# Sharing four PSUM banks among five users, and an order made from lengths taken back to back

## The chip, the cores and the metric

The kernel runs on one core of one Trainium2 chip. The metric is device time in microseconds (us) of one execution; the engines are TensorE (PE, with its weight loads as PEld), VectorE (DVE), ScalarE (ACT), GpSimd (POOL) and SyncE (SP), which here only issues DMAs. Each engine works through its own instructions in the order in which the program issues them, and waits for the others by semaphores. Before the change, three runs gave a median of 290.82 us (290.71 to 291.96).

## What is computed

Attention over 4 batches of 8 heads, 768 positions and 64 dimensions, in which each query sees only the 6 best of 24 chunks of 32 keys, and then an MLP on the 3072 tokens (512 to 2048 to 512) with an ELU between:

```python
k_min, k_max = min and max of k over each chunk of 32 keys
ub = sum over d of max(q * k_min, q * k_max)          # a bound for each query and chunk
ub = where(chunk of the query >= chunk, ub, -1e9)
top_chunks = the 6 chunks with the largest ub
scores = q @ k.T / 8, where the key's chunk is in top_chunks and key <= query
x = softmax(scores) @ v                                # 3072 x 512 after the heads are joined
h = x @ w_in                                           # 512 -> 2048
g = where(h > 0, h, exp(min(h, 0)) - 1)
out = g @ w_out                                        # 2048 -> 512
```

## The kernel before

Two heads make a pair; there are 16 pairs (the *units* u), four to a batch. Pairs are worked in halves of 384 queries (hf), and two pairs together are a quad for the selection of chunks. Each kind of step is one function that adds operations to a plan:

- `pair_prep` (line 361) for pairs 4 to 15: loads k, q and v, transposes k and q on DVE (L383, L401), takes the chunks' minima and maxima on DVE (L387, L394), and casts into the matmul operands on POOL (L506, L416). The loads of k and q go through three buffers named stage.
- `first_prep` (line 419) for pairs 0 to 3: the same with transposes on PE (L463), evicted by ACT.
- `quad_sel` (line 509): bounds by 32 small matmuls (L536), a transpose, the eighth largest value and a comparison on DVE (L553 to L573), and four copies on POOL (L583), which put the mask beside q as 24 more rows of the score matmul's operand.
- `pair_attend` (line 595): score matmuls into a double bank psS (L615), the exponential on ACT (L625), the causal triangle on POOL (L637), PV on PE into psO (L649), normalisation on DVE (L661, L664), three transposes on PE into psT (L673), and their copy into xT on ACT (L676).
- `mlp` (line 680), for each batch and half: 16 column blocks of up (L698, four matmuls each, into psH), the ELU as an exponential on ACT (L712) with a clamp (L730) and a maximum (L735) on DVE, or, in the blocks that `BOTH` names, with a second ACT operation (L717) and one DVE operation over two blocks (L723); then three row blocks of down (L747, 16 matmuls each, into psM), an eviction on ACT (L755) and the store (L759). The last batch takes the double banks for up and the class MT for down.

PSUM has eight banks. `caps` (line 190) gives S2 two double banks, and the other four single banks are one class `ps`, from which all the other users take. Each of these has a cap beside it: H (up, and the transposes of k at the start) 2, O (PV) 1, T (x^T) 2, M (down) 1, MT (transposes of q at the start, down of the last batch) 2. An operation that opens a bank takes one place of `ps` and one of its own class (`bank`, line 212), and both come free a latency after the last operation that reads it.

What sets the order of everything is `Plan.order` (line 106): a list scheduler, run when the program is made. Every operation has an engine, a length, and a priority; lower goes first. An operation may start when what it reads is written, a latency `LAT` after the writer's end, and when its buffers have places. The scheduler takes at each step the engine and operation that can start first, and among those that can start on one engine the one of lowest priority. It writes down this order, and the engines then run it as it stands: lengths and latencies in the plan set the order alone, not how long anything takes. The priorities are positions on an axis of pairs: attention of pair u at u, and half a pair later its second half (`pos`, line 269); preparation of pair u by `AHEAD` earlier (`AHEAD0` for pairs 0 to 3); selection 0.8 earlier; loads 4 earlier; the MLP of batch b from 4b + `MLAG[b]` on (`mpos`, line 275). The lengths come from `act`, `dve` and `pool` (lines 258 to 265) or stand beside an `add`. Weights are loaded by eight DMAs on POOL's queue, each behind an operation that `WHEN` names.

Of the kernel before, what the change touches and what calls it, by code (L numbers as in the profile page):

```python
# [16 lines left out]
H = 8  # L17
S = 768
# [37 lines left out]
class Plan:  # L56
# [3 lines left out]

    LAT = {"PE": 0.22, "ACT": 0.20, "DVE": 0.16, "POOL": 0.25, "SP": 2.2, "POOLQ": 2.5}

# [116 lines left out]
def kernel(  # L179
# [9 lines left out]
    nc = tc.nc  # L189
    caps = {"S2": 2, "ps": 4, "H": 2, "O": 1, "T": 2, "M": 1, "HT": 3, "MT": 2,  # L190
# [119 lines left out]
    def c_rows(i):  # L310
# [26 lines left out]
    def weights(i, gate):  # L337

        if i < 4:
            def f():  # L340
                nc.gpsimd.dma_start(out=w_in_sb[:, :, 512 * i:512 * i + 512], in_=wi3[:, :, 512 * i:512 * i + 512])
            name = ("w_in", i)
        else:
            def f():
                nc.gpsimd.dma_start(out=w_out_sb[:, 4 * i - 16:4 * i - 12, :], in_=wo3[:, 4 * i - 16:4 * i - 12, :])
            name = ("w_out", i - 4)
        add("POOL", 0.9, -20.0, f, reads=gate + ([("asked", i - 1)] if i else []), writes=[("asked", i)], lat=0.0)
        add("DMA", 3.05, -20.0, lambda: None, reads=[("asked", i)], writes=[name], lat=2.0)
# [12 lines left out]
    def pair_prep(u):  # L361
# [48 lines left out]
        def vload():  # L410
# [3 lines left out]
        fetch(1.0, 393.0, 205.0, pl + 1.2, vload, [vd], alloc=[vd])  # L414
        add("POOL", 0.09 + 0.00097 * S, pr + 1.0,
            lambda: nc.gpsimd.tensor_copy(out=tiles[vx][:, :, 0:D], in_=tiles[vd]),  # L416
            reads=[vd, "ones"], writes=[(vx, i) for i in range(2)], alloc=[vx], free=[vd])

    def first_prep(u, hf):
# [39 lines left out]
        def turn(bb, i):  # L459
# [4 lines left out]
            return f  # L464
        add("PE", 0.66, pr, turn(bk, i0), reads=[(sg, i0), "ident"], writes=[bk[0]], alloc=bk)
        for hd in range(2):
# [4 lines left out]
        for x, op in ((0, AOT.min), (1, AOT.max)):  # L471
# [10 lines left out]
            reads=[kx, (km, 0, hf)], writes=[(km, 1, hf)], free=[kx])  # L482
        add("PE", 0.66, pr + 0.05, turn(bq, i0 + 1), reads=[(sg, i0 + 1), "ident"], writes=[bq[0]], alloc=bq,
            free=[sg] if u == SPLIT[-1] else [])
# [11 lines left out]
        add("POOL", 0.09 + 0.00097 * HALF, pr + 1.0,  # L496
            lambda: nc.gpsimd.tensor_copy(
# [5 lines left out]
    def cast(pr, w, what, **kw):  # L503
        def f():
            o, i = what()
            nc.gpsimd.tensor_copy(out=o, in_=i)  # L506
        add("POOL", 0.09 + 0.00097 * w, pr, f, **kw)

    def quad_sel(g, hf):
# [5 lines left out]
        if True:  # L515
# [25 lines left out]
            for u in pairs:  # L541
# [3 lines left out]
                if hf:  # L545
                    fr += [PAIR[u]["km"]]
            add("PE", 4 * n / 2400 + 0.06, pr, ub, reads=rd, writes=[bu[0]], alloc=bu, free=fr)
            ut, = new("ubt")
# [3 lines left out]
            def t1(bu=bu, ut=ut, n=n, nh=nh, nb=nb, m0=m0):  # L552
# [6 lines left out]
            add("DVE", dve(n) + 0.16, pr, t1, reads=[bu[0]], writes=[ut], alloc=[ut], free=bu)  # L559
# [4 lines left out]
            add("DVE", 0.09 * nb + 0.07, pr, mx, reads=[ut], writes=[th], alloc=[th])  # L564
# [5 lines left out]
            add("DVE", dve(NCH * nb), pr, lt, reads=[ut, th, "kept"], writes=[sv], alloc=[sv], free=[ut, th])  # L570

# [4 lines left out]
            for j, u in enumerate(pairs):  # L576
                for odd in range(2):
                    r0 = 64 * odd + 32 * j
                    qb = PAIR[u]["qb"]

                    def put(r0=r0, odd=odd, qb=qb, c0=c0, n=n):
                        dst = tiles[qb][64:64 + NCH, :, SEL0 + c0:SEL0 + c0 + n]
                        nc.gpsimd.tensor_copy(  # L583
                            out=dst.rearrange("c h (i two x) -> c h i two x", two=2, x=32)[:, :, :, odd, :],
                            in_=tiles[st][r0:r0 + NCH, c0:c0 + n].rearrange("c (h i x) -> c h i x", h=2, x=32))
                    add("POOL", 0.12 + 0.0010 * n, pr + 0.01, put,
                        reads=[(st, hf)], writes=[(qb, hf, odd, "left")], free=[st] if hf and j and odd else [])
# [7 lines left out]
    def pair_attend(u, hf):  # L595
# [4 lines left out]
        if True:  # L600
# [4 lines left out]
            for ti, segs in enumerate(tiles_by_half[hf]):  # L605
# [5 lines left out]
                def sc(segs=segs, bs=bs):  # L611
                    p_s = tiles[bs[0]]
                    for (kb, c0, w, pc) in segs:
                        for hd in range(2):
                            nc.tensor.matmul(p_s[:, hd, pc:pc + w],  # L615
                                             lhsT=tiles[pt_["kb"]][0:64 + NCH, hd, 128 * kb:128 * kb + 128],
                                             rhs=tiles[pt_["qb"]][0:64 + NCH, hd, c0:c0 + w], start=True, stop=True)
                add("PE", 2 * wtot / 2400 + 0.02, pr, sc,
                    reads=[(pt_["kb"], i, hd) for i in range(hf + 1) for hd in range(2)]
# [22 lines left out]
            for qi, qt in enumerate(range(3 * hf, 3 * hf + 3)):  # L642
                for hd in range(2):
                    def pv(hd=hd, qi=qi, qt=qt, bo=bo, where=where):
                        po = ps(bo, [P, 2, 3, D + 1], F32)
                        for kb in range(qt + 1):
                            pt, c0, pc = where[kb]
                            off = pc + 128 * qt - c0
                            nc.tensor.matmul(po[:, hd, qi, :], lhsT=tiles[pt][:, hd, off:off + 128],  # L649
                                             rhs=tiles[pt_["vx"]][:, 6 * hd + kb, :],  # L650
                                             start=(kb == 0), stop=(kb == qt))
                    last = hd == 1 and qi == 2
                    add("PE", 0.033 * (qt + 1) + 0.02, pr, pv,
                        reads=[where[kb][0] for kb in range(qt + 1)] + [(pt_["vx"], i) for i in range(hf + 1)],
                        writes=[(bo[0], hd, qi)], alloc=bo if (hd, qi) == (0, 0) else [],
                        free=(held + ([pt_["vx"]] if hf else [])) if last else [])
# [3 lines left out]
            add("DVE", 0.19, pr,  # L660
                lambda rc=rc, bo=bo: nc.vector.reciprocal(out=tiles[rc], in_=ps(bo, None, None)[:, :, :, D:D + 1]),  # L661
# [8 lines left out]
            def xt(on=on, bx=bx):  # L670
                px = ps(bx, [P, HALF], BF16)
                for n in range(3):
                    nc.tensor.transpose(px[:, 128 * n:128 * n + 128], tiles[on][:, n, :, :], ident_b)  # L673
            add("PE", 0.18, pr, xt, reads=[on, "ident_b"], writes=[bx[0]], alloc=bx, free=[on])
            add("ACT", act(HALF), pr,
# [4 lines left out]
    def mlp(b, hf):  # L680
        tail = b == B - 1
        if True:
# [3 lines left out]
            for fc in range(0, NFC, step):  # L686
# [6 lines left out]
                def up(view=view, fc=fc, c0=c0):  # L693
                    for i in range(step):
                        ph = view()[:, i, :]
                        for kk in range(NKK):
# [3 lines left out]
                                             start=(kk == 0), stop=(kk == NKK - 1))  # L700
                add("PE", step * 4 * (HALF / 2400 + 0.003), pr, up,
                    reads=[("w_in", fc // 4)] + [(XT[4 * b + kk], hf) for kk in range(NKK)],
# [12 lines left out]
                if both:  # L715
# [12 lines left out]
                    continue  # L728
                add("DVE", 0.21 + 0.00037 * step * HALF, pr,
                    lambda e=e, t=t: nc.vector.tensor_scalar(  # L730
# [8 lines left out]
            for tt in range(3):  # L739
                bm = bank("MT" if tail else "M")  # L740
                for part in range(4):
                    pr = mpos(b, hf) + 2 + 2 * (4 * tt + part) / 12

                    def down(bm=bm, tt=tt, part=part, gt=gt):
                        pm = ps(bm, [P, DMODEL], F32)
                        for fc in range(4 * part, 4 * part + 4):
                            nc.tensor.matmul(pm, lhsT=tiles[gt][:, fc, 128 * tt:128 * tt + 128],  # L747
                                             rhs=w_out_sb[:, fc, :], start=(fc == 0), stop=(fc == NFC - 1))
                    add("PE", 4 * (512 / 2400 + 0.003), pr, down,
                        reads=[("w_out", part)] + [(gt, fc) for fc in range(4 * part, 4 * part + 4)],  # L750
                        writes=[(bm[0], part)], alloc=bm if part == 0 else [],
                        free=[gt] if tt == 2 and part == 3 else [])
# [86 lines left out]
```

## Time and profile before

| | us |
|---|---|
| median of three runs | 290.82 |
| the profiled execution, as timed | 291.4 |
| its span, first to last instruction | 289.3 |
| PE idle in the span | 26.4 |
| first matmul starts | 4.30 |
| last exponential of the attention ends, about | 240 |

The profile is that of one execution. A row of a group gives line, engine, operation, what it writes and reads, and the count, then the busy time and the mean ns of one; behind the second bar stands the idle time of the engine just before these instructions, with what ended it. Matmuls and operations of ACT and DVE overlap their neighbours by some of their length, so that a mean is longer than the time from one start to the next. A row of waits gives who waited for whom, the total, the number of times and the longest. A row of stage sums gives the busy time of each engine between two times. The chain of work that ended last is, by engine, 61% PE, 16% DVE, 8% POOL, 7% ACT.

### The profile page before, as it was taken

Reading aid. Unit: us, or ns where it says so; the run is one execution under the profiler, and the core shown is the slowest. Engines: PE = TensorE matmul, PEld = TensorE weight load, DVE = VectorE, ACT = ScalarE, POOL = GpSimd, SP = SyncE. Lnnn points to the kernel's source line nnn. Section 1 sums busy time; section 2 is a strip of 40 time slices with the busy share of each in tenths; the row PEclk is TensorE's granted clock in tenths of the full one; section 3 lists DMA queues with packets and bytes.
Section 4 is the critical chain, followed back from the end, with each engine's and each line's share of the span. In section 5 each row is a group of like instructions: output and inputs, shape, how many; then the busy total and the mean of one; then the engine's idle time right before and its main releaser. Section 6 shows DMA issues by size and latency. Waiting matters only on the chain.

```text
span 289.3 us, 6815 instructions
## 1 busy us (share of the span) xinstructions
PE 262.9 (91%) x2512; PEld 156.1 (54%) x2512; DVE 204.3 (71%) x542; ACT 202.2 (70%) x373; POOL 140.3 (49%) x238
## 2 busy tenths in 40 slices
PE   3686789969999999988889999999999999999994
PEld 2455456634565655645555656565566555555542
DVE  7835755799999978989999576756684517665620
ACT  3759599955898695898968987785869583443421
POOL 4678893384997699797759541521142010000000
PEclk9999799999999999999999999999999999999999
DMA  8878999999699979999734010001101010010011
GB/s 163 187 166 170 214 196 207 201 133 182 120 182 152 177 109 203 145 196 119 130 73 91 5 39 36 2 36 39 36 3 37 22 53 2 36 39 36 36 73 73
DMA packets 120992, 29.79 MB, mean 103 GB/s; under 512 B 113792, under 2 KB 117888, under 8 KB 120960
## 3 DMA queue, kind: packets, MB, share of 16 engines
q1 hardware_dynamic: 115136, 24.78, 46.9%
q0 software_dynamic: 4224, 4.19, 8.9%
q10 hardware_dynamic: 1600, 0.39, 0.7%
q8 instruction: 19, 0.31, 0.5%
q14 instruction: 13, 0.11, 0.1%
HBM read 27.26 MB, written 6.29 MB: 116 GB/s over the span
## 4 chain that ended last, share of the span: by engine, by line
PE 61%; DVE 16%; POOL 8%; ACT 7%; issue 4%; DMA 2%; DVEq 0%; POOLq 0%; ACTq 0%
PE psM L747 16%; PE psH L698 14%; PE psS L615 8%; PE psS L698 7%; PE psMT L747 7%; PE psO L649 5%; POOL rhs L583 3%; ACT pt L625 3%; PE psS L536 2%; DMA w_out_sb<-in_moe_w_out_dram 2%; DVE t L730 2%; POOL lhs L506 2%; DVE kx L387 1%; DVE thr L563 1%; POOL pt L637 1%
## 5 line engine op out<-in xcount | busy, mean ns | idle before, releaser
L625 ACT ACTIVATE pt<-psS 128x768 bf16<-128x768 f32 x112 | 90.1, 836 | 9.7 <-PE psS L615 9.3
L698 PE MATMUL psH<-xT,w_in_sb 128*128 128x384 bf16 x384 | 76.4, 325 | 4.2 <-DVE gT L735 3.2
L747 PE MATMUL psM<-w_out_sb,gT 128*128 128x512 bf16 x288 | 73.3, 379 | 0.4 <-DVE gT L723 0.3
L698 PEld LDWEIGHTS <-w_in_sb 128*128 128x128 bf16 x512 | 47.7, 97 | 36.6 <-issue 5.8
L712 ACT ACTIVATE e<-psH 128x384 f32<-128x384 f32 x96 | 48.2, 509 | 25.0 <-PE psH L698 24.3
L637 POOL TENSOR_SCALAR_AFFINE_SELECT pt<-pt 128x256 bf16<-128x256 bf16 x64 | 33.7, 531 | 53.7 <-ACT pt L625 44.9
L615 PE MATMUL psS<-rhs,lhs 88*128 88x384 bf16 (+2 forms) x288 | 52.3, 295 | 5.0 <-POOL rhs L583 3.8
L730 DVE TENSOR_SCALAR t<-e 128x384 bf16<-128x384 f32 (+1 forms) x64 | 33.6, 531 | 30.8 <-ACT e L712 30.4
L747 PEld LDWEIGHTS <-gT 128*128 128x128 bf16 x384 | 35.7, 97 | 35.6 <-DVE gT L723 1.1
L583 POOL COPY rhs<-selt 24x192 bf16<-24x192 bf16 (+1 forms) x64 | 30.6, 478 | 19.8 <-DVE selt L573 16.4
L615 PEld LDWEIGHTS <-lhs 88*128 88x128 bf16 x288 | 26.9, 99 | 21.3 <-issue 7.6
L649 PE MATMUL psO<-vext,pt 128*128 128x65 bf16 x672 | 32.0, 195 | 4.9 <-POOL pt L637 4.8
L506 POOL CAST rhs<-qt 64x768 bf16<-64x768 f32 (+1 forms) x40 | 29.5, 736 | 13.6 <-ACT qt L486 7.3
L649 PEld LDWEIGHTS <-pt 128*128 128x128 bf16 x672 | 28.4, 99 | 13.5 <-POOL pt L637 6.5
L723 DVE SCALAR_TENSOR_TENSOR gT<-e,t 128x768 bf16<-128x768 f32 x24 | 24.4, 1018 | 13.6 <-ACT t L717 13.4
L712 ACT ACTIVATE e<-psS 128x768 f32<-128x768 f32 x16 | 13.0, 810 | 21.4 <-PE psS L698 21.4
L735 DVE TENSOR_TENSOR gT<-t,psH 128x384 bf16<-128x384 bf16 x48 | 25.7, 542 | 1.9
L506 POOL CAST lhs<-kt 64x768 bf16<-64x768 f32 x24 | 23.4, 974 | 6.7 <-PE psS L615 3.0
L717 ACT ACTIVATE t<-psH 128x384 bf16<-128x384 f32 x48 | 24.6, 517 | 0.0
L698 PE MATMUL psS<-xT,w_in_sb 128*128 128x384 bf16 x128 | 23.4, 326 | 0.0
L747 PE MATMUL psMT<-w_out_sb,gT 128*128 128x512 bf16 x96 | 22.2, 379 | 0.0
L676 ACT ACTIVATE xT<-psT 128x384 bf16<-128x384 bf16 x32 | 16.3, 509 | 6.3 <-PE psT L673 6.2
(52 smaller groups left out, 268.1 us busy)
## 6 DMA issues: line engine op xcount, KB each, us to landing
out_dram<-osb SPq DMA_DIRECT2D x24, 256.0 KB, 2.0
stage<-in_k_dram SPq DMA_DIRECT2D x48, 96.0 KB, 4.0
stage<-in_q_dram SPq DMA_DIRECT2D x48, 96.0 KB, 3.5
vd<-in_v_dram SPq DMA_DIRECT2D x24, 192.0 KB, 3.8
w_in_sb<-in_moe_w_in_dram POOLq DMA_DIRECT2D x4, 512.0 KB, 8.2
w_out_sb<-in_moe_w_out_dram POOLq DMA_DIRECT2D x4, 512.0 KB, 8.6
gT<-in_k_dram SPq DMA_DIRECT2D x16, 96.0 KB, 2.7
gT<-in_v_dram SPq DMA_DIRECT2D x16, 96.0 KB, 2.6
```

The source lines that it names most:

```text
L506: nc.gpsimd.tensor_copy(out=o, in_=i)
L583: nc.gpsimd.tensor_copy(out=dst.rearrange("c h (i two x) -> c h i two x", two=2, x=32)[:, :, :, odd, :], in_=tiles[st][r0:r0 + NCH, c0:c0 ...
L615: nc.tensor.matmul(p_s[:, hd, pc:pc + w], lhsT=tiles[pt_["kb"]][0:64 + NCH, hd, 128 * kb:128 * kb + 128], rhs=tiles[pt_["qb"]][0:64 + NCH, ...
L625: lambda bs=bs, pt=pt, wtot=wtot: nc.scalar.activation(out=tiles[pt][:, :, 0:wtot], in_=tiles[bs[0]][:, :, 0:wtot], func=AF.Exp, scale=SCALE),
L637: nc.gpsimd.affine_select(out=a, in_=a, compare_op=AOT.is_ge, fill=0.0, base=0, pattern=pat, channel_multiplier=-1)
L649: nc.tensor.matmul(po[:, hd, qi, :], lhsT=tiles[pt][:, hd, off:off + 128], rhs=tiles[pt_["vx"]][:, 6 * hd + kb, :], start=(kb == 0), stop= ...
L698: nc.tensor.matmul(ph, lhsT=w_in_sb[:, kk, f0:f0 + 128], rhs=tiles[XT[4 * b + kk]][:, c0:c0 + HALF], start=(kk == 0), stop=(kk == NKK - 1))
L712: lambda e=e, view=view, i=i, w=w: nc.scalar.activation(out=tiles[e][:, i:i + w], in_=view(), func=AF.Exp),
L717: lambda t=t, view=view, i=i: nc.scalar.activation(out=tiles[t][:, i:i + 1], in_=view(), func=AF.Relu),
L730: lambda e=e, t=t: nc.vector.tensor_scalar(out=tiles[t][:, 0:step], in0=tiles[e][:, 0:step], scalar1=1.0, scalar2=1.0, op0=AOT.min, op1=AO ...
L735: lambda t=t, view=view, fc=fc, gt=gt: nc.vector.tensor_tensor(out=tiles[gt][:, fc:fc + step, :], in0=tiles[t][:, 0:step], in1=view(), op= ...
L747: nc.tensor.matmul(pm, lhsT=tiles[gt][:, fc, 128 * tt:128 * tt + 128], rhs=w_out_sb[:, fc, :], start=(fc == 0), stop=(fc == NFC - 1))
```

## The change

No operation is added or taken away. `caps` gives up to three banks to up, one to PV, one to x^T and two to down; the pool of four stays. The lengths and latencies of the plan are replaced, most by shorter ones, the clamp (L730) and the first fills by longer ones. `AHEAD` goes from 1.2 to 1.6, and `MLAG` of batches 1 to 3 from 3.5 to 3.0. The emitted instructions are the same; their order on each engine, and the banks and buffers that they use, are what the scheduler makes of the new numbers.

```diff
-MLAG = (2.0, 3.5, 3.5, 3.5)
-AHEAD = 1.2
+MLAG = (2.0, 3.0, 3.0, 3.0)
+AHEAD = 1.6
...
-    LAT = {"PE": 0.22, "ACT": 0.20, "DVE": 0.16, "POOL": 0.25, "SP": 2.2, "POOLQ": 2.5}
+    LAT = {"PE": 0.21, "ACT": 0.17, "DVE": 0.13, "POOL": 0.08, "SP": 2.2, "POOLQ": 2.5}
...
-    caps = {"S2": 2, "ps": 4, "H": 2, "O": 1, "T": 2, "M": 1, "HT": 3, "MT": 2,
+    caps = {"S2": 2, "ps": 4, "H": 3, "O": 1, "T": 1, "M": 2, "MT": 2,
...
     def act(n):
-        return 0.11 + 0.00082 * n
+        return 0.062 + 0.00082 * n
     def dve(n, rate=1):
-        return 0.12 + 0.00104 * n / rate
+        return 0.065 + 0.00104 * n / rate
     def pool(n):
-        return 0.16 + 0.00115 * n
+        return 0.15 + 0.00088 * n
...
-    add("DVE", 0.5, -9.9, c_fill, writes=["fill"])
+    add("DVE", 0.85, -9.9, c_fill, writes=["fill"])
-    add("DVE", 0.8, -9.0, c_zero, writes=["zero"])
+    add("DVE", 1.05, -9.0, c_zero, writes=["zero"])
```

The other lengths are written into `add` one by one, old on the left, new on the right:

```
weights (POOL issue)   0.9                      0.79
cast, v copy (POOL)    0.09 + 0.00097 n         0.13 + 0.00096 n
mask copy (POOL)       0.12 + 0.0010 n          0.20 + 0.00095 n
turn (PE)              0.66                     0.64
ub (PE)                4 n / 2400 + 0.06        0.22 + 0.002 n
ub transpose (DVE)     dve(n) + 0.16            dve(n) + 0.03
eighth largest (DVE)   0.09 nb + 0.07           0.078 nb
comparison (DVE)       dve(24 nb)               0.02 + 0.00125 * 24 nb
scores (PE)            2 w / 2400 + 0.02        2 w / 2400 + 0.01
PV (PE)                0.033 (qt + 1) + 0.02    0.0325 (qt + 1) + 0.005
reciprocal (DVE)       0.19                     0.115
x^T (PE)               0.18                     0.17
up (PE), each matmul   HALF / 2400 + 0.003      0.1625
clamp (DVE)            0.21 + 0.00037 n         0.32 + 0.00021 n
down (PE), each matmul 512 / 2400 + 0.003       0.2165
```

More of the change, by code (lines that the diff above doesn't have):

```diff
@@ L346, in weights @@
             name = ("w_out", i - 4)
-        add("POOL", 0.9, -20.0, f, reads=gate + ([("asked", i - 1)] if i else []), writes=[("asked", i)], lat=0.0)
+        add("POOL", 0.79, -20.0, f, reads=gate + ([("asked", i - 1)] if i else []), writes=[("asked", i)], lat=0.0)
         add("DMA", 3.05, -20.0, lambda: None, reads=[("asked", i)], writes=[name], lat=2.0)
@@ L414, in pair_prep @@
         fetch(1.0, 393.0, 205.0, pl + 1.2, vload, [vd], alloc=[vd])
-        add("POOL", 0.09 + 0.00097 * S, pr + 1.0,
+        add("POOL", 0.13 + 0.00096 * S, pr + 1.0,
             lambda: nc.gpsimd.tensor_copy(out=tiles[vx][:, :, 0:D], in_=tiles[vd]),
@@ L464, in turn @@
             return f
-        add("PE", 0.66, pr, turn(bk, i0), reads=[(sg, i0), "ident"], writes=[bk[0]], alloc=bk)
+        add("PE", 0.64, pr, turn(bk, i0), reads=[(sg, i0), "ident"], writes=[bk[0]], alloc=bk)
         for hd in range(2):
@@ L482, in first_prep @@
             reads=[kx, (km, 0, hf)], writes=[(km, 1, hf)], free=[kx])
-        add("PE", 0.66, pr + 0.05, turn(bq, i0 + 1), reads=[(sg, i0 + 1), "ident"], writes=[bq[0]], alloc=bq,
+        add("PE", 0.64, pr + 0.05, turn(bq, i0 + 1), reads=[(sg, i0 + 1), "ident"], writes=[bq[0]], alloc=bq,
             free=[sg] if u == SPLIT[-1] else [])
@@ L495, in first_prep @@
                  reads=[qt], writes=[(qb, hf, hd)], alloc=[] if hf or hd else [qb])
-        add("POOL", 0.09 + 0.00097 * HALF, pr + 1.0,
+        add("POOL", 0.13 + 0.00096 * HALF, pr + 1.0,
             lambda: nc.gpsimd.tensor_copy(
@@ L506, in f @@
             nc.gpsimd.tensor_copy(out=o, in_=i)
-        add("POOL", 0.09 + 0.00097 * w, pr, f, **kw)
+        add("POOL", 0.13 + 0.00096 * w, pr, f, **kw)
     def quad_sel(g, hf):
@@ L546, in quad_sel @@
                     fr += [PAIR[u]["km"]]
-            add("PE", 4 * n / 2400 + 0.06, pr, ub, reads=rd, writes=[bu[0]], alloc=bu, free=fr)
+            add("PE", 0.22 + 0.002 * n, pr, ub, reads=rd, writes=[bu[0]], alloc=bu, free=fr)
             ut, = new("ubt")
@@ L558, in t1 @@
                     nc.vector.memset(flat[0:64, i0:i0 + 34 * (nb // 2 - 1) + 1:34], CAUSNEG)
-            add("DVE", dve(n) + 0.16, pr, t1, reads=[bu[0]], writes=[ut], alloc=[ut], free=bu)
+            add("DVE", dve(n) + 0.03, pr, t1, reads=[bu[0]], writes=[ut], alloc=[ut], free=bu)
             def mx(ut=ut, th=th, nb=nb, m0=m0):
@@ L563, in mx @@
                     nc.vector.max(out=tiles[th][:, i, :], in_=tiles[ut][:, i, 0:m0 + 2 * (i % (nb // 2)) + 2])
-            add("DVE", 0.09 * nb + 0.07, pr, mx, reads=[ut], writes=[th], alloc=[th])
+            add("DVE", 0.078 * nb, pr, mx, reads=[ut], writes=[th], alloc=[th])
             def lt(ut=ut, th=th, sv=sv, nb=nb):
@@ L569, in lt @@
                     in1=tiles[th][:, 0:nb, TOPK - 1:TOPK].to_broadcast([P, nb, NCH]), op=AOT.is_lt)
-            add("DVE", dve(NCH * nb), pr, lt, reads=[ut, th, "kept"], writes=[sv], alloc=[sv], free=[ut, th])
+            add("DVE", 0.02 + 0.00125 * NCH * nb, pr, lt, reads=[ut, th, "kept"], writes=[sv], alloc=[sv], free=[ut, th])
             def t2(sv=sv, n=n, c0=c0):
@@ L585, in put @@
                             in_=tiles[st][r0:r0 + NCH, c0:c0 + n].rearrange("c (h i x) -> c h i x", h=2, x=32))
-                    add("POOL", 0.12 + 0.0010 * n, pr + 0.01, put,
+                    add("POOL", 0.20 + 0.00095 * n, pr + 0.01, put,
                         reads=[(st, hf)], writes=[(qb, hf, odd, "left")], free=[st] if hf and j and odd else [])
@@ L617, in sc @@
                                              rhs=tiles[pt_["qb"]][0:64 + NCH, hd, c0:c0 + w], start=True, stop=True)
-                add("PE", 2 * wtot / 2400 + 0.02, pr, sc,
+                add("PE", 2 * wtot / 2400 + 0.01, pr, sc,
                     reads=[(pt_["kb"], i, hd) for i in range(hf + 1) for hd in range(2)]
@@ L652, in pair_attend @@
                     last = hd == 1 and qi == 2
-                    add("PE", 0.033 * (qt + 1) + 0.02, pr, pv,
+                    add("PE", 0.0325 * (qt + 1) + 0.005, pr, pv,
                         reads=[where[kb][0] for kb in range(qt + 1)] + [(pt_["vx"], i) for i in range(hf + 1)],
@@ L659, in pair_attend @@
             o_all = [(bo[0], hd, qi) for hd in range(2) for qi in range(3)]
-            add("DVE", 0.19, pr,
+            add("DVE", 0.115, pr,
                 lambda rc=rc, bo=bo: nc.vector.reciprocal(out=tiles[rc], in_=ps(bo, None, None)[:, :, :, D:D + 1]),
@@ L673, in xt @@
                     nc.tensor.transpose(px[:, 128 * n:128 * n + 128], tiles[on][:, n, :, :], ident_b)
-            add("PE", 0.18, pr, xt, reads=[on, "ident_b"], writes=[bx[0]], alloc=bx, free=[on])
+            add("PE", 0.17, pr, xt, reads=[on, "ident_b"], writes=[bx[0]], alloc=bx, free=[on])
             add("ACT", act(HALF), pr,
@@ L700, in up @@
                                              start=(kk == 0), stop=(kk == NKK - 1))
-                add("PE", step * 4 * (HALF / 2400 + 0.003), pr, up,
+                add("PE", step * 4 * 0.1625, pr, up,
                     reads=[("w_in", fc // 4)] + [(XT[4 * b + kk], hf) for kk in range(NKK)],
@@ L728, in mlp @@
                     continue
-                add("DVE", 0.21 + 0.00037 * step * HALF, pr,
+                add("DVE", 0.32 + 0.00021 * step * HALF, pr,
                     lambda e=e, t=t: nc.vector.tensor_scalar(
@@ L748, in down @@
                                              rhs=w_out_sb[:, fc, :], start=(fc == 0), stop=(fc == NFC - 1))
-                    add("PE", 4 * (512 / 2400 + 0.003), pr, down,
+                    add("PE", 4 * 0.2165, pr, down,
                         reads=[("w_out", part)] + [(gt, fc) for fc in range(4 * part, 4 * part + 4)],
```

## The prediction, made before the changed kernel had run

> **What bounds the kernel now.** I read the totals of the page first, then stage sums cut where the row of tenths changes, then what PE waited for in the first two stages, then the groups.
>
> ```profile
> span 289.3 us, 6815 instructions
> PE 262.9 (91%) x2512; PEld 156.1 (54%) x2512; DVE 204.3 (71%) x542; ACT 202.2 (70%) x373; POOL 140.3 (49%) x238
> ```
>
> PE is busy 262.9 of 289.3 us, so 26.4 us are idle. The stage sums (columns: elapsed time, then PE, PEld, DVE, ACT, POOL busy, the clock, DMA) say where:
>
> ```profile
> 0.00:50.00 50.00, 36.91 (x392) 24.72 (x393) 31.41 (x119) 35.66 (x69) 34.60 (x78) 0.97 1.05 186
> 50.00:150.00 100.00, 90.84 (x1025) 54.50 (x1024) 92.30 (x233) 80.05 (x152) 75.24 (x108) 1.00 0.98 155
> 150.00:240.00 90.00, 89.55 (x859) 53.66 (x858) 57.65 (x163) 69.95 (x132) 30.48 (x52) 1.00 0.10 32
> 240.00:286.00 46.00, 45.64 (x242) 23.27 (x240) 22.97 (x31) 16.20 (x23) 0.00 (x0) 1.00 0.11 40
> 286.00:289.30 3.30, 0.00 (x0) 0.00 (x0) 0.00 (x0) 0.32 (x1) 0.00 (x0) 0.89 0.21 79
> ```
>
> Idle PE is 13.1, 9.2, 0.45, 0.36 and 3.3 us. From 150 us to the last matmul PE hardly stops, and the change removes no matmul. So the end moves only by what PE loses before 150 us, unless a new hole opens later. Between 50 and 150 us DVE is at 92.3 of 100 us: it prepares pairs 4 to 15 there, beside batches 0 and 1 of the MLP, and falls to 57.65 of 90 us once that is done. Engines run in order, so PE's losses are the waits of the planner's order:
>
> ```profile
> PE psH L698 <- DVE gT L735: 3.2, 3, 1.3
> PE psO L649 <- POOL pt L637: 3.1, 7, 1.0
> PE psT L673 <- DVE on L664: 0.7, 1, 0.7
> PE psS L615 <- ACT pt L625: 0.6, 2, 0.4
> ```
>
> These are the largest waits of PE between 50 and 150 us (total, times, longest). In the first row an up matmul waits until DVE has read an older psH: that is a wait for a bank. psO behind POOL is a wait for data, a masked pt that the order took for ready. Before 50 us the waits are another sort: 5.0 us for the first k to land and 3.8 us (longest 3.0) for the selection copied by POOL (L583).
>
> **The change, part by part.** It adds and removes no instruction; it deals banks out anew and makes another order. No trace of before shows that order, so every part has two ends.
>
> *Third bank for up.* The three waits of the first row are 1.32, 1.15 and 0.70 us in the timeline. With a third bank, one more up of four matmuls (0.65 us in the chain) can run before the bank is needed: what is left is 0.67, 0.50 and 0.05, so 3.2 becomes 1.2 and the gain is 2.0 us. Ends: nothing, when the freed place is filled with more ups and the wait only comes one up later; 3.8 us, which is this row and the two of 0.3 us each for psH behind ACT.
>
> *Second bank for down.* A psM is held through four parts (4 x 0.86 us) and the eviction, mean 614 ns (L755). In this trace no wait of PE names psM and an eviction, since other work stands between two downs. So I take nothing; the ends are nothing and, at 0.6 us for each of the 7 evictions of L755 between 50 and 150 us, 4.2 us of freedom that PE could only use where it idles, which is in the same 9.2 us.
>
> *One bank for x^T instead of two.* It is held for three transposes and a copy: 0.33 us and 509 ns (L676), with the gaps about 1 us, 32 times. No wait names psT for its bank. Two users seldom meet within 1 us; I charge 0.4 us (one meeting in the sixteen halves of that stage), ends nothing and 16 x 0.5 = 8 us, if every copy stood in the way. All four single banks are one pool as before: three ups and one PV leave none for down and x^T.
>
> *New lengths.* The mean of a group includes the end of its pipeline; back to back the starts lie closer. In the timeline one pt exponential of 0.87 us starts at 50.46 and the next ACT operation at 51.15, 0.69 us later; the old length for 768 elements is 0.74, the new 0.69. A 128x384 operation is followed after 0.37 us (old 0.425, new 0.377). Summed over all operations, the old lengths give DVE 205 and ACT 202 us, the new 187 and 184; PE stays at 255 and POOL at 136. So the old order was made for DVE and ACT slower than they are, and places PE's attention work later than its data are ready; with true lengths it should stall less on data. The data waits between 50 and 150 us are 3.1 + 0.7 + 0.6 + 0.4 + 0.3 = 5.1 us. I take half, 2.5 us; ends nothing and 5.1. POOL's latency falls from 0.25 to 0.08 us, and psO behind POOL is the largest data wait, so this part can also lose: seven waits lengthened by 0.17 are 1.2 us.
>
> *AHEAD 1.2 to 1.6, MLAG 3.5 to 3.0.* Both go ahead of attention by nearly the same step, so among themselves preparation gains 0.1 of a pair on batches 1 to 3 and 0.4 on batch 0, whose lag stays 2.0. A pair costs DVE two transposes, two reductions and a subtraction, 3.64 us by the new lengths: 0.4 x 3.64 = 1.5 us of DVE work go before the MLP's in the stage where DVE has 7.7 us left. PE feels part of it: 0.5 us, ends nothing and 1.5. The loads move along on SP's queue. Their places come free when DVE has transposed (SP waits 11.2 us there behind DVE, none of DVE's waits is for a load), so I price the queue at nothing; what hides it is DVE's own backlog.
>
> *Before 50 us and at the end.* The start hangs on landings and on the chain through selection, which keep their work; I take nothing, ends 1.5 us each way (half of the longest wait, 3.0). The end, eviction and store behind the last matmul, stays 3.3 us.
>
> **The sum**: -2.0 - 2.5 + 0.4 + 0.5 = -3.6 us. The profiled execution took 291.4 us, its span 289.3. So 291.4 - 3.6 = 287.8 us for an execution like it, and as the median of the runs (290.82) is 0.6 us lower, 287.2 us.
>
> **A row that speaks against the lengths.** DVE's clamp t<-e (L730) on 384 elements is planned at 0.40 us. By shape it takes
>
> ```profile
> L730 DVE TENSOR_SCALAR t<-e 128x384 bf16<-128x384 f32 x13 | 5.4, 412 | 7.2 <-ACT e L712 7.2
> L730 DVE TENSOR_SCALAR t<-e 128x384 bf16<-128x384 f32 x16 | 11.3, 720 | 0.7 <-ACT e L712 0.7
> ```
>
> The first row is 200 to 240 us, where POOL is nearly idle; the second 60 to 150 us, where POOL casts: 0.31 us more each. A length from an undisturbed place is 16 x 0.31 = 5 us short in the stage where DVE is full. The Trainium skill, "SBUF — State Buffer", section "Who interferes with whom", says that such an instruction with a constant can take a port pair that DVE shares with GpSimd, and that whichever comes second blocks until the other is through. By that rule the stretch follows casts wherever they go, and the trace agrees as far as it goes, 720 against 412 ns.
>
> **Rivals.**
> - *The lock (slower).* The new order counts on 18 us of DVE time that the old did not, but the clamps take 5 us more than planned in that stage, and more of batches 0 and 1 stands beside the casts since the MLP is earlier. It decides when DVE's 7.7 us are used up: 5 + 1.5 + the casts' own stretch (974 ns for lhs against a planned 0.87, 24 of them: 2.5) is 9.0. PE then loses that and gets no data wait back: -2.0 + 0.4 + 4 = +2.4, about 293 us. Chance 0.15.
> - *Banks (slower).* Three ups hold three of four banks, each until a full DVE has read it (waits of about 1.07 us in before), and PV or x^T of the next half finds none; the attention that feeds the next batch gets late. It decides from the point where PE has no other ready work. Six of sixteen halves at 1.07 us are 6.4 us, less the 2.5 of the lengths: about 294.5 us. For it: four banks carry five kinds. Against it: the planner knows the banks and puts other work in between. Chance 0.17.
> - *No difference.* The waits change names, since DVE at 92% feeds PE all the same in that stage: 290.8 us, chance 0.15.
> - *More is recovered.* Bank waits 3.8, data waits 5.1 and 1.5 at the start go: 290.8 - 10.4, at best 280.5; about 282.5 where a fifth of it stays. Chance 0.11.
> - The forecast, 287.2 us (284 to 289.3): chance 0.42.
>
> **How the numbers follow.** Half a per cent, 1.5 us, is about what a measurement of this kernel can tell from no change: 289.4 to 292.3 us is "same". Forecast and full recovery give 0.53 faster, the no-difference case 0.15, the two slower rivals 0.32. With about one in ten left out on each side, the range goes from 282.5, where recovery is nearly full, to 295, just over the banks' rival.
>
> **What would show it.** Right: from 150 us on PE again without holes; PE idle between 50 and 150 us near 5.6 us; the psH row behind DVE near 1.2 us; the last matmul about 3.6 us sooner. Wrong: psT, psO or psM waiting for banks (rival two); DVE over 95% with L730 above 720 ns and PE behind DVE (rival one); or a hole after 150 us, because attention came late and a batch of the MLP lacks its x^T, which nothing in this trace prices, as there is no such hole in it. The start could also move by more than 1.5 us, if the shorter lengths let the order ask before the loads have landed.

## The result and the profile after

The changed kernel takes 293.28 us, the median of 16 runs (292.18 to 294.56); before took 291.32 us beside it. The ratio is 1.0067, 95% interval 1.0047 to 1.0086: **slower by 2 us**, where a gain of 3.6 us, to 287.2, was forecast. The time lies in the range, but on the other side of no change. Single executions that took over 1.5% longer than the quickest of the same kernel are left out of the times and ratios below. The profiled execution took 292.27 us, at the quick end of its runs:

```profile
span 290.5 us, 6802 instructions
PE 260.4 (90%) x2483; PEld 154.5 (53%) x2512; DVE 207.7 (72%) x542; ACT 201.3 (69%) x373; POOL 139.2 (48%) x238
```

The stage sums, with the same columns as before (29 of PE's 2512 matmul records are missing from this trace, about half of them between 50 and 150 us, so a little of PE's idle time is not real):

```profile
0.00:50.00 50.00, 34.03 (x384) 23.06 (x385) 31.74 (x117) 34.13 (x69) 33.89 (x77) 0.90 1.06 186
50.00:150.00 100.00, 91.60 (x982) 54.53 (x997) 91.62 (x223) 81.89 (x156) 70.48 (x104) 1.00 0.89 151
150.00:240.00 90.00, 88.52 (x863) 52.41 (x874) 59.67 (x169) 66.13 (x125) 33.73 (x56) 1.00 0.13 37
240.00:286.00 46.00, 45.79 (x269) 24.44 (x273) 24.65 (x34) 18.55 (x26) 1.04 (x2) 1.00 0.11 40
286.00:290.50 4.50, 0.50 (x2) 0.06 (x1) 0.00 (x0) 0.60 (x1) 0.00 (x0) 1.00 0.15 58
```

Before 50 us PE idles 16.0 instead of 13.1 us. Between 50 and 150 us it idles 8.4 instead of 9.2 us, but DVE's full stage now lasts to 160 us. Cut there, PE is busy for the same time in both; this is before, then the changed kernel:

```profile
50.00:160.00 110.00, 100.84 (x1094) 60.28 (x1093) 102.27 (x252) 88.71 (x170) 82.80 (x117) 1.00 0.92 147
```

```profile
50.00:160.00 110.00, 100.84 (x1079) 59.70 (x1088) 101.56 (x251) 88.73 (x170) 77.20 (x113) 1.00 0.85 144
```

PE's waits between 50 and 150 us in the changed kernel have other names. All rows of this view add up to 7.4 us, against 8.9 before; without psH behind DVE they are 5.8 us (and 0.2 without a name) against 5.7. The largest are:

```profile
PE psT L673 <- DVE on L664: 1.7, 3, 0.8
PE psH L698 <- DVE gT L735: 1.4, 2, 1.1
PE psS L615 <- POOL rhs L583: 1.4, 2, 1.2
PE psO L649 <- POOL pt L637: 0.7, 2, 0.4
PE psS L615 <- ACT pt L625: 0.7, 1, 0.7
PE psO L649 <- ACT xT L676: 0.5, 1, 0.5
PE psS L615 <- DVE ubt L553: 0.5, 1, 0.5
```

What is new stands at the start. These are the timeline's PE rows of the changed kernel around its second long hole (start, length, what; the hole ahead in brackets):

```profile
29.71 0.56 PE L536 MATMUL psS<-qt,km 64*32 64x192 f32 x16
...
34.68 0.50 PE L673 MATMUL psT<-ident_b,on 128*128 128x128 bf16 x3 [3.30 <-DVE on L664]
35.11 0.89 PE L536 MATMUL psS<-qt,km 64*32 64x192 f32 x16
```

PE waits 3.30 us for DVE's normalisation of pair 3. Before had two groups of bounds (L536) ahead of that x^T, and its hole was 1.00 us:

```profile
32.96 0.56 PE L536 MATMUL psS<-qt,km 64*32 64x192 f32 x16
33.31 0.82 PE L536 MATMUL psS<-qa,km 64*32 64x192 f32 x16
35.13 0.34 PE L673 MATMUL psT<-ident_b,on 128*128 128x128 bf16 x3 [1.00 <-DVE on L664]
```

In the changed kernel 16 matmuls of one shape that took 0.56 us ahead of the hole take 0.89 us behind it. The clock says why (the last column but two, in two stretches of the changed kernel):

```profile
10.00:20.00 10.00, 5.84 (x70) 3.53 (x62) 4.82 (x20) 5.67 (x12) 6.75 (x16) 0.71 0.82 185
30.00:40.00 10.00, 6.63 (x99) 3.58 (x84) 7.64 (x42) 4.71 (x11) 8.28 (x15) 0.83 1.42 214
```

PE ran at half clock from 14.2 to 21.1 and from 34.7 to 38.1 us. The record starts at the first change of the clock, so the 1.00 that a trace shows ahead of it says nothing: in before, whose record starts at 22.3 us, a transposition ahead of that takes as long as at half clock and one behind it does not.

```profile
21.37 0.88 PE L463 MATMUL psH<-ident_f,gT 128*128 128x128 f32 x3
24.45 0.55 PE L463 MATMUL psH<-ident_f,gT 128*128 128x128 f32 x3
```

So before ran at half clock up to 22.3 us and again from 29.1 to 32.5, the changed kernel up to 10.8 us and in the two stretches above: in the first 50 us that is 21.4 us of before from the first matmul on, and 16.7 of the changed kernel. An estimate from these traces, PE's busy time halved where the clock was: by 50 us before has done 28.5 us of work at full clock and the changed kernel 26.9, so it is 1.7 us behind there. It idles 2.9 us more and loses 1.2 us less by the clock. The 16 runs fall into groups by the mean clock: 292.2 to 292.6 us at 0.980 to 0.982, 293.2 to 293.6 at 0.968 to 0.971, 294.2 to 294.6 at 0.968.

### The profile page after: what moved, and what is told of

The parts are those of the page before. It is cut to its first block, busy times and chain, and to the rows that moved or that the text cites. A ratio compares the mean times of both kernels' runs of the same rounds, so it can differ in the third digit from the quotient of the medians.

```text
span 290.5 us, 6802 instructions
## 1 busy us (share of the span) xinstructions
PE 260.4 (90%) x2483; PEld 154.5 (53%) x2512; DVE 207.7 (72%) x542; ACT 201.3 (69%) x373; POOL 139.2 (48%) x238
## 4 chain that ended last, share of the span: by engine, by line
PE 49%; DVE 24%; ACT 14%; issue 5%; POOL 3%; DMA 3%; SPq 0%; DVEq 0%; POOLq 0%; ACTq 0%
PE psM L747 12%; PE psH L698 10%; PE psS L698 7%; ACT pt L625 7%; PE psMT L747 7%; PE psS L615 6%; PE psO L649 3%; ACT e L712 3%; DVE thr L563 2%; DVE t L730 2%; DVE gT L723 2%; DVE gT L735 2%; DMA vd<-in_v_dram 2%; DVE kx L387 2%; DVE km L387 2%
## 5 line engine op out<-in xcount | busy, mean ns | idle before, releaser
L747 PE MATMUL psM<-w_out_sb,gT 128*128 128x512 bf16 x263 | 69.4, 379 | 1.8 <-ACT t L717 0.3
L712 ACT ACTIVATE e<-psH 128x384 f32<-128x384 f32 x96 | 48.2, 530 | 24.0 <-PE psH L698 22.8
L637 POOL TENSOR_SCALAR_AFFINE_SELECT pt<-pt 128x256 bf16<-128x256 bf16 (+1 forms) x64 | 33.3, 527 | 60.0 <-ACT pt L625 58.7
L615 PE MATMUL psS<-rhs,lhs 88*128 88x384 bf16 (+2 forms) x288 | 51.4, 296 | 7.2 <-POOL rhs L583 5.0
L730 DVE TENSOR_SCALAR t<-e 128x384 bf16<-128x384 f32 (+1 forms) x64 | 32.2, 506 | 24.9 <-ACT e L712 24.4
L583 POOL COPY rhs<-selt 24x192 bf16<-24x192 bf16 (+1 forms) x64 | 29.8, 465 | 22.0 <-DVE selt L573 18.4
L615 PEld LDWEIGHTS <-lhs 88*128 88x128 bf16 x288 | 26.9, 99 | 23.7 <-issue 10.4
L506 POOL CAST rhs<-qt 64x768 bf16<-64x768 f32 (+1 forms) x40 | 31.1, 777 | 15.4 <-DVE qt L401 7.8
L723 DVE SCALAR_TENSOR_TENSOR gT<-e,t 128x768 bf16<-128x768 f32 x24 | 27.0, 1124 | 12.1 <-ACT t L717 12.0
L712 ACT ACTIVATE e<-psS 128x768 f32<-128x768 f32 x16 | 13.0, 812 | 19.1 <-PE psS L698 19.1
L506 POOL CAST lhs<-kt 64x768 bf16<-64x768 f32 x24 | 21.5, 896 | 6.9 <-DVE kt L383 5.1
```

The costliest lines, as they stand in the source:

```text
L583: nc.gpsimd.tensor_copy(out=dst.rearrange("c h (i two x) -> c h i two x", two=2, x=32)[:, :, :, odd, :], in_=tiles[st][r0:r0 + NCH, c0:c0 ...
L615: nc.tensor.matmul(p_s[:, hd, pc:pc + w], lhsT=tiles[pt_["kb"]][0:64 + NCH, hd, 128 * kb:128 * kb + 128], rhs=tiles[pt_["qb"]][0:64 + NCH, ...
L637: nc.gpsimd.affine_select(out=a, in_=a, compare_op=AOT.is_ge, fill=0.0, base=0, pattern=pat, channel_multiplier=-1)
L712: lambda e=e, view=view, i=i, w=w: nc.scalar.activation(out=tiles[e][:, i:i + w], in_=view(), func=AF.Exp),
L723: lambda e=e, t=t, fc=fc, gt=gt: nc.vector.scalar_tensor_tensor(out=tiles[gt][:, fc - 1:fc + 1, :], in0=tiles[e], scalar=1.0, in1=tiles[t] ...
L730: lambda e=e, t=t: nc.vector.tensor_scalar(out=tiles[t][:, 0:step], in0=tiles[e][:, 0:step], scalar1=1.0, scalar2=1.0, op0=AOT.min, op1=AO ...
```

## Which part of the change it is

Theory A put the loss at the start and on the new lengths, B on the banks, C on the priorities. Each part was run alone and in pairs. Times are medians; ratios are to before run beside each and lie near the ratio of the mean times, so that they differ a little from the quotient of two medians.

**Lengths and latencies alone.**

```diff
 banks, MLAG and AHEAD of before; LAT, act(), dve(), pool() and all other lengths of the change
```

> Before with the new lengths and latencies alone; banks, AHEAD and MLAG as before. Theory A (the loss lies in the first 50 us, where the new lengths make an order with longer holes of PE, 3.6 and 3.3 us, and the clock falls): this alone gives most of the loss, +1 to +2 us against before, with a hole of over 3 us behind the normalisation of pair 3 between 30 and 36 us. Theory B (banks): no loss here, -1 to 0 us. Theory C (priorities): no loss here, -1 to +0.5 us.

300.24 us, ratio 1.0286 (1.0258 to 1.0315). The size is far over what any theory said, and the place is wrong too: the start is that of the changed kernel, with the same hole of 3.3 us, but PE is busy only 97.88 us between 50 and 160 us, 6.8 us of this stretch are at half clock, and with two banks for up PE waits there for

```profile
PE psH L698 <- DVE gT L735: 4.6, 5, 1.7
PE psO L649 <- POOL pt L637: 2.2, 3, 0.9
PE psT L673 <- DVE on L664: 1.2, 3, 0.5
```

**Banks alone, priorities alone.**

```diff
-"H": 2, "O": 1, "T": 2, "M": 1
+"H": 3, "O": 1, "T": 1, "M": 2
```

> Before with the new shares of the banks alone (up 3, x^T 1, down 2). Theory A: within 0.7 us of before, the start hardly changed. Theory B (three ups hold the banks that PV and x^T need): +1.5 us or more, with waits of psO or psT for banks between 50 and 160 us. Theory C: within 0.7 us.

290.08 us, ratio 0.9950 (0.9930 to 0.9971): a gain. B falls. The row of psH behind DVE is 1.3 us.

```diff
-MLAG = (2.0, 3.5, 3.5, 3.5)
-AHEAD = 1.2
+MLAG = (2.0, 3.0, 3.0, 3.0)
+AHEAD = 1.6
```

> Before with AHEAD 1.6 and MLAG 3.0 alone. Theory A: within 0.7 us of before, since nothing before about 45 us is moved by them, and what PE loses between 50 and 150 us is set by the work of DVE there. Theory C (preparation and MLP pushed ahead of attention, which ends some 7 us later in the changed kernel): +1.5 us or more, with the loss between 50 and 160 us. Theory B: within 0.7 us.

288.13 us, ratio 0.9887 (0.9861 to 0.9913). C falls, and A's "within 0.7 us" with it. PE gains 2.7 us between 50 and 160 us, with DVE as full as before:

```profile
50.00:160.00 110.00, 103.51 (x1111) 61.04 (x1110) 102.14 (x254) 90.67 (x175) 81.42 (x117) 1.00 0.90 146
```

**Pairs of parts**, edited as above.

> The changed kernel with the old lengths and latencies: banks and priorities alone. If the parts add up (banks -1.4 us, priorities -3.3 us alone): -4.7 us, 286.7 us, with PE losing under 8 us between 50 and 150 us. If both gains are the same waits of psH behind DVE, found twice: -3.3 us, 288.1 us. If the order is a matter of luck at each change: anywhere between -4.7 and +3 us.

293.89 us, ratio 1.0086 (1.0052 to 1.0120): two gains together are a loss.

> New lengths and new banks, AHEAD and MLAG as before. With the lengths alone PE waited 5.0 us for psH behind DVE. If the third bank takes most of that, +4 us against before (the lengths' +8.8 less 4 to 5); if the parts only add up, +7.4 us; the rest of the way to the changed kernel's +2 us is then what the priorities give here.

295.24 us, ratio 1.0134 (1.0103 to 1.0165).

> New lengths and AHEAD 1.6, MLAG 3.0, with the banks as before: the last of the eight ways to make the change in part. If parts add up (lengths +8.8, priorities -3.3 us alone): +5.5 us, 297 us; from the changed kernel (+2.0) without the banks' -1.4: +3.4 us. Theory L: neither number holds, anything between 288 and 300 us.

295.64 us, ratio 1.0120 (1.0086 to 1.0154). The start goes with the lengths: x^T of pair 3 waits 3.3 us for DVE in all four kernels that have the new ones, and 0.8 to 1.3 us in the four that have the old ones. The total does not follow, and nothing adds up. In per cent, the banks give -0.5, the priorities -1.1, the lengths +2.9; banks with priorities +0.9, lengths with banks +1.3, with priorities +1.2, all three +0.7. No part of the change has a worth that it keeps when another is set beside it.

## Slack in the lengths, or a new deal

Two theories were left: S, the too long old lengths are slack that keeps PE fed; L, any change of a number deals the greedy list anew, and before is a good deal. The first pair of runs moved all lengths along the line from old to new (new - old = 1), the others one constant by 5 ns.

```diff
 lengths and latencies: old + 0.5 * (new - old)
```

> Before, with each length and latency half way between the old and the new value; banks and priorities as before. If the slack in the old lengths is what keeps PE fed (theory S): a part of the lengths' loss that grows with the cut, +3 to +6 us. If any change of lengths deals the list anew and the +8.8 us are one unlucky draw (theory L): anything from -3 to +9 us, in no order with the cut.

294.59 us, ratio 1.0118 (1.0079 to 1.0157).

```diff
 lengths and latencies: old - 0.5 * (new - old)
```

> Before, with each length and latency moved the other way, by half the distance from the new to the old value beyond the old one (a 128x384 ACT operation 0.449 us instead of 0.425, POOL's latency 0.335 instead of 0.25); banks and priorities as before. Theory S: no loss, -3 to 0 us. Theory L: anything, as likely slower as faster.

299.31 us, ratio 1.0269 (1.0244 to 1.0294): more slack is as bad as none. S falls.

```diff
-        return 0.11 + 0.00082 * n
+        return 0.115 + 0.00082 * n
```

> Before with one number moved by next to nothing: the constant of ACT's lengths 0.115 instead of 0.110 us, 1% of a 128x384 operation. Theory L (each change of numbers deals the greedy list anew; before is a lucky draw): a time that differs by 1 us or more, rather slower, up to 300 us. Theory S (the cut in the lengths matters, by its size): within 0.7 us of before.

293.85 us, ratio 1.0073 (1.0043 to 1.0102). Five ns in the plan cost as much as the whole change. On DVE the two traces part after the 58th instruction, where a reduction (L473) and a reciprocal (L661) change places; 237 of DVE's 542 places then hold another kind of instruction, and only the last 59 are alike again.

> The same 5 ns on top of AHEAD 1.6 and MLAG 3.0 alone. Theory L: the gain of 3.3 us of the priorities alone is a draw too and does not last: 290 to 297 us. If the priorities have a worth of their own: 287.5 to 289 us, or at least 3 us less than the run of before with the 5 ns.

With the same edit: 299.45 us, ratio 1.0242 (1.0203 to 1.0280). The gain of the priorities does not outlive 5 ns.

```diff
 changed kernel, act(): 0.062 -> 0.067 and, in another run, 0.057
```

> The changed kernel with the constant of ACT's lengths at 0.067 instead of 0.062 us. Theory L: the changed kernel's 293.3 us is one draw from a spread of some 288 to 300 us that every setting shares, so 1 us or more away from it, either way. If the change has a worth of its own that a few ns do not touch: 292.5 to 294.3 us.

293.38 us, ratio 1.0046 (1.0026 to 1.0065).

> The changed kernel with the constant of ACT's lengths at 0.057 instead of 0.062 us. Theory L: as with the 5 ns more, and in no order with it: anywhere between 288 and 300 us. If the change has a worth of its own: 292.5 to 294.3 us.

295.56 us, ratio 1.0128 (1.0097 to 1.0159). The first lies as near to the changed kernel as a worth of its own would have it, the second does not. Fourteen orders of the same instructions, before's among them, take 0.989 to 1.029 of before's time, and eleven are slower than it. Of the four moves by 5 ns one did nothing clear of the noise (0.2%), and the others moved the time by 0.6, 0.7 and 3.6%. Theory L stands: before is among the better deals, and the change's +0.7% is within what 5 ns do.

## What a bad deal is made of: holes, and the clock behind them

Theory G: a stretch in which PE idles much is followed by 3.41 us at half clock. The holes of the start were filled with matmuls into the bank that the waiting ones then overwrite.

```diff
+ first scores:           28 matmuls ident_b x ident_b, 128 columns, into psS
+ x^T of pair 3, half 0:  28 transposes of ident_b into psT
```

> The changed kernel with 28 matmuls of 128 columns more ahead of the first score matmul and 28 transposes more ahead of the x^T of pair 3, first half, each into the bank that the real ones then overwrite: they stand in the two holes of 3.6 and 3.3 us and keep PE busy there. If the holes cost by the clock that falls after them: 0.7 to 2 us less than the changed kernel, 291.3 to 292.5 us, a mean granted clock of 0.985 or more in all runs, and runs that differ by less than 0.8 us. If only the holes themselves cost: the same time as the changed kernel, 293.3 us, or up to 1 us more for the added work that juts out.

290.20 us, ratio to before 0.9951 (0.9935 to 0.9967), runs from 289.62 to 291.29 us: 3.1 us less than the changed kernel, with more work for PE, and 1.1 us under what the clock was expected to give at most. The runs still differ by 1.7 us. The same stretches as above, now of the filled kernel:

```profile
10.00:20.00 10.00, 6.91 (x103) 5.18 (x95) 5.08 (x22) 6.05 (x12) 6.70 (x16) 0.86 0.74 168
30.00:40.00 10.00, 8.16 (x121) 5.50 (x108) 8.43 (x43) 6.16 (x13) 8.62 (x17) 1.00 1.42 215
```

The clock between 30 and 40 us is full. Before and the priorities' kernel got the like: the 28 matmuls, 12 and 26 more ahead of two PV groups of pair 2, and 12 transposes ahead of the x^T.

> Before with the same added matmuls at the same places; its order is that of the priorities' run up to about 45 us. Theory G: its half-clock windows up to 22.3 us and from 29.1 to 32.5 us go, 0.7 to 1.7 us less than before, about 290 us; so that the changed kernel filled (290.2 us) and before filled are alike, and the change's loss is its two longer holes at the start. Without G: 291.3 us or a little more.

290.53 us, ratio 0.9951 (0.9930 to 0.9973). Filled, the two kernels are level in time, but this does not show that the clock made the difference between them. A filled kernel has the order of the unfilled one (the added lines only shift its line numbers), so their traces can be laid side by side. These are an up matmul of the changed kernel, then the same one filled; then an up and the first down of before, and the same two of before filled:

```profile
40.59 0.81 PE L698 MATMUL psH<-xT,w_in_sb 128*128 128x384 bf16 x4
```

```profile
38.64 0.81 PE L704 MATMUL psH<-xT,w_in_sb 128*128 128x384 bf16 x4
```

```profile
42.19 0.81 PE L698 MATMUL psH<-xT,w_in_sb 128*128 128x384 bf16 x4
45.05 1.02 PE L747 MATMUL psM<-w_out_sb,gT 128*128 128x512 bf16 x4
```

```profile
40.41 0.81 PE L708 MATMUL psH<-xT,w_in_sb 128*128 128x384 bf16 x4
44.41 1.02 PE L757 MATMUL psM<-w_out_sb,gT 128*128 128x512 bf16 x4 [1.19 <-DMA w_out_sb<-in_moe_w_out_dram]
```

Filling brings the changed kernel forward by 1.9 us and before by 1.8: as far as the fills take the half clock of the start away, it cost both alike in these traces. Then filled before has caught up with a DMA, waits 1.19 us for the weights of down, and keeps 0.6 us; the filled changed kernel has no such wait. So the half clock is a cost of both starts, and in these traces the filled kernels are level by a wait for weights. What the changed kernel has more of than before is idle time. (Its trace is from the quick end of its runs; in the others the clock may take more.)

> Before with AHEAD 1.6 and MLAG 3.0 alone, and added matmuls in the holes of the first 36 us (28 ahead of the first scores, 12 and 26 ahead of two PV groups of pair 2, 12 transposes ahead of the x^T of pair 3), each into the bank that the real ones then overwrite. Theory G (a window of 3.4 us in which PE idles much is followed by 3.4 us at half clock): the half-clock windows up to 20.8 us and from 31.1 to 37.9 us go, and 1 to 2 us with them: 286 to 287.2 us. Without G: 288.1 us or a little more.

287.65 us, ratio 0.9853 (0.9827 to 0.9878): the quickest version here, quicker than both kernels. Its median is 0.5 us over what was expected. Set against before beside each, it is 0.3% below the unfilled one, with intervals that overlap, so that a gain by the filling is not shown here; it too waits for the weights of down, 0.7 us.

Then the middle, in the order of the priorities with 5 ns more, which has five half-clock windows after 45 us.

```diff
+ first scores of pair 4:  50 matmuls ident_b x ident_b
+ x^T of pair 3, half 1:   36 transposes of ident_b       (first of the two runs only)
```

> The order of the priorities with 5 ns more (299.5 us), and added matmuls in its two longest holes of the middle: 36 transposes ahead of the x^T of pair 3, second half (a hole of 2.3 us, PE behind DVE), and 50 matmuls of 128 columns ahead of the first scores of pair 4 (3.2 us, behind POOL), each into the bank that the real ones overwrite. The half-clock windows there are 63.3 to 70.1 and 73.6 to 80.4 us. If the windows follow from the holes (theory G): both go, and 4 to 6 us with them, 293.5 to 295.5 us. If the holes alone cost: 299.5 us or up to 1 us more.

299.06 us, ratio 1.0258 (1.0216 to 1.0299), against 293.5 to 295.5 us by theory G: inconclusive. The transposes waited with the real ones and stood behind their hole of 2.31 us, as work of 2.9 us more. Without them:

> The order of the priorities with 5 ns more (299.5 us), with the 50 added matmuls ahead of the first scores of pair 4 alone: the 36 added transposes of the run before stood behind the same wait as the real ones, did not fill their hole and put 2.9 us of work behind it. Theory G: the half-clock window of 6.8 us behind the 3.2 us hole goes (73.6 to 80.4 us), and 2 to 3.4 us with it: 296 to 297.5 us. If the hole alone costs: 299.5 us or a little more.

296.49 us, ratio 1.0187 (1.0159 to 1.0215), where the unfilled order had 1.0242 (1.0203 to 1.0280). The hole and what follows it, unfilled and then filled:

```profile
74.67 1.44 PE L615 MATMUL psS<-rhs,lhs 88*128 88x384 bf16 x6 [3.16 <-POOL rhs L583]
```

```profile
71.41 2.96 PE L615 MATMUL psS<-ident_b 128*128 128x128 bf16 x50
74.68 0.81 PE L618 MATMUL psS<-rhs,lhs 88*128 88x384 bf16 x6 [0.32 <-POOL rhs L583]
```

The scores start at the same time, since POOL is no sooner, but take 0.81 instead of 1.44 us. So a part of what a bad order costs is not its holes but the clock behind them, here about 0.55 of 2.4%. The rest of these 7 us, and what makes one order poorer in holes than another, is not settled. No single wait is the largest in all the slow orders.

## Why the prediction was wrong, point by point

- **The bound** was right: PE has no holes after the stage in which DVE is full, and all is decided before. That stage ends when DVE's work is done, and reaches to 160 us here.
- **Third bank for up**: the number came out, the mechanism is not shown. The row of psH behind DVE was put at 1.2 us; it is 1.4, and 1.3 with the banks alone, which gain 0.5%, 1.4 us, against 2.0 less 0.4. But the row is 1.0 us with two banks and the new priorities, and 3.3 us with three banks in the changed kernel with 5 ns more. It moves with the deal as much as with the bank, so the match may be luck.
- **New lengths, -2.5 us**: the step that failed. It said that an order made from true lengths stalls less on data, by half of 5.1 us. Between 50 and 150 us the waits of PE other than for psH stayed, 5.1 us before and 5.8 now, and at the start the new lengths made one longer, 3.30 us for the x^T of pair 3 instead of 1.00. The lengths alone cost 2.9%, half of the way 1.2%, and the way back 2.7%: the order is not the better the truer the lengths. One length was measured, and the new plan is nearer to it: in before, idle DVE starts 0.523 us (median of 20) after the start of the ACT exponential L712 of 384 elements that it waits for; the plan now says 0.377 + 0.17, and said 0.425 + 0.20.
- **AHEAD and MLAG, +0.5 us**: by themselves they gain 1.1%, and with 5 ns more they cost 2.4%; a price for this edit by itself has no meaning here. The working also had a step the wrong way round: preparation moves 0.4 of a pair ahead and the MLP 0.5, so on batches 1 to 3 the MLP gains 0.1 on preparation.
- **The sum**: it added parts. The eight combinations show that they don't add, so a sum of this sort could not have come out right but by chance. That the time lies in the range is luck as well: six of the other orders lie above it, since it was made for the mechanisms that I could name and not for the spread of the list. Two figures of the rivals do not follow from their rows: 290.8 - 10.4 is 280.4, not 280.5, and the 4 us that the lock takes from PE have no source; its own 9.0 us against 7.7 left give 1.3.
- **Before 50 us, nothing, 1.5 us each way**: wrong, and here the 2 us lie. PE idles 2.9 us more in the profiled start, and by the estimate above it is 1.7 us of work behind at 50 us. Landings and selection kept their work, as I said, but the order of the new lengths has the x^T of pair 3 ahead of bounds that stood before it and kept PE busy. The clock I left out altogether; it costs the start, but before's start as well.
- **The lock**: not it. DVE is at 91.6 of 100 us, and between 60 and 150 us L730 is shorter than before (720 ns), not longer:

```profile
L730 DVE TENSOR_SCALAR t<-e 128x384 bf16<-128x384 f32 x15 | 9.2, 616 | 0.1
```

- **The banks' rival**: not it; psT waits for its data, 1.7 us behind DVE, not for a bank, and the banks alone gain. **No difference**, by waits that change names, is what happened between 50 and 160 us, with 100.84 us of PE in both.

## What to carry to other kernels

Where a greedy list sets the order of engines that run in order, price the parts of a change to it by a spread, not by a sum: move one number by 5 ns in the kernel before, and look how far the time goes. Here that was 0.2 to 3.6%, where the change was 0.7%, and the best of several deals was worth more than truer numbers. A hole of PE costs its own length and the half clock that can follow it; some added matmuls in a hole that must be there (28 to 50 here) can keep the clock, and the gain lasts only until PE meets the next wait.

## What the runs showed of the hardware

All traces but that of the run told inconclusive were cut into the windows of 3.41 us in which the recorded clock changes. Up to the last matmul, PE's busy share in the 41 windows at full clock that were followed by half clock was 0 to 0.62; of the 1319 that were followed by full clock none had under 0.54. (Where the last matmul falls into a window, there are three with 0.45 to 0.48 that full clock followed, so this is no sharp limit.) So a window that is 40 to 45% idle can lose the next one's clock, and one long hole is not needed. The kernel with banks and priorities shows it in two neighbouring windows, cut so:

```profile
70.88:74.29 3.41, 1.11 (x6) 0.67 (x7) 3.41 (x20) 1.75 (x4) 1.68 (x3) 1.00 1.02 121
74.29:77.70 3.41, 3.19 (x13) 1.65 (x12) 3.17 (x5) 2.11 (x3) 3.09 (x7) 0.50 0.29 64
```

The holes in the first are 0.96 and 1.37 us. The Trainium skill, "TensorE: Matmul & The Clock Gate", section "HAM oscillation — how this bites in real kernels", gives as the rule that gaps of PE over about 3.4 us are to be avoided. Taken as a limit it is too wide here, and the measurement decides: gaps of less than half of that were enough, when they fell into one window. Where the windows fall differs between traces: the first recorded change comes at 10.8 us in the changed kernel and at 10.5 us with the lengths alone, whose start is the same. The changed kernel's runs, which differ by up to 2.4 us, fall into groups by their clock; that the place of the windows is the cause is likely but not shown.
